# Another written-out order for the attention steps, with two more tiles of exponentials and the splitting of the maxima moved to GpSimd

## Chip, core and metric

The kernel runs on one core of a Trainium2 chip. The metric is the device time of one execution in microseconds (us). Engines are called as the profile calls them: PE (matmuls), DVE (VectorE), ACT (ScalarE), POOL (GpSimd), SP (the queue that issues most DMAs). Engines run side by side, each one its own instructions in order, and they wait for each other by semaphores.

## What is computed

From one input x of 2048 tokens by 512 features the kernel computes a gate, a sliding-window attention and an MLP, and mixes them:

```python
def _A_ref(x, wqkv, wo):        # 32 heads of 16, window of 256
    qkv = (lambda x, *d: x.transpose(*d))((x @ wqkv).reshape(B, S, 3, H, Dh), 2, 0, 3, 1, 4)
    scores = jnp.einsum("bhqd,bhkd->bhqk", q, k) * (Dh ** -0.5)
    mask = (idx[:, None] - idx[None, :] >= 0) & (idx[:, None] - idx[None, :] < W)
    scores = jnp.where(mask[None, None], scores, -1e9)
    p = _softmax(scores, axis=-1)
    o = jnp.einsum("bhqk,bhkd->bhqd", p, v)
    return (lambda x, *d: x.transpose(*d))(o, 0, 2, 1, 3).reshape(B, S, D) @ wo

def _B_ref(x, w1, b1, w2, b2):  # layer norm, 512 -> 1792, gelu, -> 512
    h = _gelu(jnp.einsum("bsd,df->bsf", _layernorm(x), w1) + b1)
    return jnp.einsum("bsf,fd->bsd", h, w2) + b2

g = _sigmoid((x * gate_w).sum(-1, keepdims=True))
return g * a + (1 - g) * b
```

All products are made with numbers split into a high and a low part, so that one product is three matmuls (or, in the scores, one matmul over stacked rows of high and low parts).

## The kernel before, in words

There are three stages, and PE has matmuls in all of them.

**Projections (to about 158 us).** q, k and v are made from x; q and k go through DRAM into "stacks", the tiles `q` and `k` of two heads per half, whose rows hold high and low parts. Here too the first maxima of the attention are made, while DVE and POOL prepare the normalised input `y` of the MLP.

**Attention mixed with the first MLP layer (about 158 to 520 us).** The 32 heads are done in eight passes of four heads (two tiles `q`, `k` with two heads each). PE's order in this stage is a string written out by hand, `ORDER`, with a letter for each step; `run` takes the letters one after the other:

- **S** (`s_pair`, L311): the scores of 128 queries with up to 384 keys, for two heads (two matmuls that run side by side, L322). DVE then masks two edges into one (`copy_predicated`, L331) and takes the row maxima (`tensor_reduce`, L332). For the first two blocks of a pass another DVE operation does it (L328).
- After the second S of every fourth block `put_max` (L336) splits four blocks' negated maxima into a high and a low part (L340, L341), transposes them on DVE (L342), writes them to DRAM (`md`, L352, one tick later) and reads them back as two more rows of `q` (L350, three ticks later). A tick is one step of a clock of the program, which `block` moves on at each T with `pr` 0. The rows of `k` that meet these rows of `q` hold 1.0 (L181), so that the matmul itself subtracts the maximum.
- **T** (`st_pair`, L357): the same scores transposed, keys by queries, with the maximum subtracted (L366). ACT takes the exponential into a tile `p` (L368), and POOL zeroes the corners outside the window (`affine_select`, L370, two for a full T). One tile `p` serves the two T of a block of keys; five are there.
- **P** (`pv`, L377): probabilities times v for 256 queries (32 matmuls of 32 columns in the trace, 16 for the first P of a pass, L385). ACT copies the result out (L121, in the last ones DVE, L392). A P reads the tiles `p` of its own two blocks of keys and of the two blocks before.
- **f** (`fill`, L655): one step, two matmuls side by side, of the first MLP layer (`mlp1_unit`, L561, matmul L575). 24 such steps make a unit of 128 hidden features by 1024 tokens; ACT copies its two halves out, and it goes to DRAM as `hp`.

PSUM, where matmuls write, has four places in this stage, the tiles `b0` to `b3` (two banks each). `ring` hands them out: the unit of the MLP holds one through its 24 steps, and S, T and P take the other three in turn. So the place that an S has written is free for the third S, T or P behind it, and that one's matmul waits until DVE (or ACT) has emptied it.

**Second MLP layer and output (from about 520 us).** The rest of the f, the second layer (L783), the output projection (L762) and the mix.

SP issues the loads and stores in the order of the program: weights of the MLP at each unit's end, stacks of the next pass (L309) and the transfers of `put_max` by ticks.

Of the kernel before, what the change touches and what calls it, by code (L numbers as in the profile page):

```python
# [17 lines left out]
ALU = mybir.AluOpType  # L18
# [11 lines left out]
NB = S // 128  # L30
# [4 lines left out]
EPS = 1e-5  # L35
NEG = -3.0e38
U8 = mybir.dt.uint8
ORDER = ("fSfTffSPffTfSffTfSffTfTfffSfTffSffSfffSPSffTfSffTfSffTfffTSPSfSfTfffTfffTSfTfffSfSPSTfTSfTffffSTPSTf"
         "TffSffTfSffTPSfTfTfffSfTffSffSPSfTfffTfSfTfffSfTPTfSfTfffTfSfTffSffTSfffSPTSfTffSffTPTSffTfSfTfSffSP"
         "SfTfSffTfTfSTfffTfSfSfPTSffTfSfTfSffTPTSfTffSfTfSffTPTSfTffTffSfTffSffSPSfTSfffTfSffTfSffTfffSTPTSff"  # L40
         "TfSffTfSffffSfSPTffTfSffTfffSfTPSfTfSfffTfSffTfSffTffSffSPSTffSffTfTffSfTfffTffSPTfSfTffSfffTfSfffSP"
         "TfSfTffSfTffTfSPTfSfTffSffTfSffTfSffTffSffSPTSfTfffTfSPSffTfSffTfSffTffSffTfSffTffSffSPTSTfffSffTPTf"
         "SfTffSffTSffTfSffSPTfSfTffTfffSfSPSffTfSffTfSffTfSfffTSffTfffSTPSfTfSffTfSffSPTSfTffSffTfSffTfffTTPT"
         "fTfSffTfffTfSPTSfTffSffSPSfTSfffTfSffTffTfSfTfffTfSPSfTffSffTffSffSPTSfTfffTfSfTfffSfTPTSfTffSffTfSf"
         "fTfSffTfSffSPTSfTfffSfTfffTfSPTfSfTfffSffTfffSTPTSfTfffSfSPSffTffTfSffTffSffTfSffTfSffffSfTffSffSPSf"
         "TfffTfSfTffSffTPTfSfTffSfffTfSffTfSfffSPTfSffTfffTfSPTfSfTfffSfTffSffTfSffTffSffSPTSfTfffSfTPTfSfTff"
         "SffTfffSTPTfSffTfSffTfSfffSPTSffTfSfTfSffTfSffTSffSPTSffTfSffTffTfSfTffSfSPTfSfTffSffTTfffSPTfSffTfS"
         "ffTffTfSfffSfffSPTfSfTffSffTfSffTfSfffSPTfSfTffTffSfTfffSfSPTSTffffTSPTSfTfffTfSfTffTffSPTSfTffSffTS"
         "ffTfSffSPTSTfffSffTPTSfTffSffTSffTfSffSPSTfSTSTfTffTPTTffffTfPTfffTffTfffTffTPTffTffffTfTPTTfffffTTP"
         "TfT")  # L50
LAG = 6


# [1 line left out]
def gated_mix_kernel(ctx, tc: tile.TileContext, xt, x2, wqk, wv, wo, xa, gw, w1, w2, b1, b2, out):  # L55
    nc = tc.nc
    dve, act, pool, pe, sp = nc.vector, nc.scalar, nc.gpsimd, nc.tensor, nc.sync
# [5 lines left out]
    def nm(s):  # L63
        uid[0] += 1
        return f"{s}_{uid[0]}"
# [10 lines left out]
    def get(key, tag, bufs, shape, dt=F32):  # L76
        return left[key].tile(list(shape), dt, name=nm(tag), tag=tag, bufs=bufs)
# [48 lines left out]
    def after(k, fn):  # L126
        todo.setdefault(step[0] + k, []).append(fn)
# [49 lines left out]
    def masks():  # L177
        for t in qs + ks:
            pool.memset(f32(t[:32]), 0.0)
        for k in ks:  # L180
            pool.memset(f32(k[96:128]), 1.0)  # L181
        one = small("scr", 2, (128, 256), BF16)
        pool.memset(one, 1.0)
        pool.affine_select(out=one[:, :128], in_=one[:, :128], pattern=[[-1, 128]], base=0, channel_multiplier=1,
                           compare_op=ALU.is_ge, fill=0.0)
        for e in range(2):
            pool.tensor_copy(tri[:, e], one[:, :128])
        pool.memset(wide, 0.0)
        pool.affine_select(out=wide[:, 128:], in_=wide[:, 128:], pattern=[[-1, 128]], base=0, channel_multiplier=1,
                           compare_op=ALU.is_ge, fill=NEG)  # L190
# [145 lines left out]
    def put_max(p, a):  # L336
        mx = mxs[p][:, :, :, a:a + 4]
        m = small("nm", 2, (128, 2, 2, 2, 4), F32R)
        ms = small("ms", 2, (128, 32))
        dve.tensor_scalar(m[:, 0], mx, -1.0, None, op0=ALU.mult)  # L340
        dve.scalar_tensor_tensor(out=m[:, 1], in0=mx, scalar=-1.0, in1=f32(m[:, 0]), op0=ALU.mult, op1=ALU.subtract)  # L341
        dve.transpose(ms, f32(m).rearrange("p a b c d -> p (a b c d)"))  # L342
        md = dram.tile([2, 2, 2, 4, 128], F32R, name=nm("md"))

        def rest():
            done.add(("m", p, a // 4))
            for pr in range(2):
                for e in range(2):
                    src = view(md, [2048, 2], [1, 512], off=(2 * pr + e) * 512)
                    sp.dma_start(f32(qs[pr][62 + 50 * e:64 + 50 * e, a * 128:a * 128 + 512]), f32(src))  # L350

        after(1, lambda: sp.dma_start(f32(view(md, [32, 4], [128, 32], [1, 32])), ms))  # L352
        after(2 if (p, a) == (7, 12) else 3, rest)

    pts, acc = {}, {}

    def st_pair(p, kb, pr):  # L357
        w = min(NB - kb, 3) * 128
        assert ("m", p, (kb * 128 + w - 1) // 512) in done
        if pr == 0:  # L360
            pts[p, kb] = get("work", "p", 5, (128, 4, 384))
        pt = pts[p, kb][:, 2 * pr:2 * pr + 2]
        o = two()
        for e in range(2):
            r, k = ((0, 64), (64, 114))[e]
            pe.matmul(o[:, e, :w], ks[pr][r:k, kb * 128:kb * 128 + 128], qs[pr][r:k, kb * 128:kb * 128 + w],  # L366
                      start=True, stop=True)
        act.activation(pt[:, :, :w], o[:, :, :w], AF.Exp, scale=0.25)  # L368
        for a, sgn, b in ((0, 1, 0), (256, -1, -1))[:1 + (w == 384)]:
            pool.affine_select(out=pt[:, :, a:a + 128], in_=pt[:, :, a:a + 128], pattern=[[0, 2], [sgn, 128]],  # L370
                               base=b, channel_multiplier=-sgn, compare_op=ALU.is_ge, fill=0.0)
# [5 lines left out]
    def pv(p, j, last):  # L377
        flush()
        a = two()[:, 0]
        parts = ((-1, 0, 128, 256), (-2, 0, 256, 128), (0, 0, 0, 256), (1, 128, 0, 128))[0 if j else 2:]  # L380
        for n, (d, at, fr, w) in enumerate(parts):
            kb = 2 * j + d
            for h in range(4):
                v = (4 * p + h) * VW
                pe.matmul(a[32 * h:32 * h + 32, at:at + w], vs[:, kb, v:v + 32], pts[p, kb][:, h, fr:fr + w],  # L385
                          start=n == 0, stop=n == len(parts) - 1, skip_group_check=True, tile_position=(0, 32 * h))
        if j % 2 == 0:
            acc[p] = t2()
        s = acc[p]
        o = j % 2 * 256  # L390
        if last:
            dve.tensor_copy(s[:, o:o + 256], a[:, :256])  # L392
        else:
            copy(s[:, o:o + 256], a[:, :256])
        if j % 2:
            to = osc[p, :, (j - 1) * 256:(j + 1) * 256]
            if lt:
                after(1, lambda: sp.dma_start(to, s))
            else:
                act.dma_start(to, s)  # L400
# [263 lines left out]
    early = []  # L664
    lt = [(p, kb, pr) for p in range(8) for kb in range(NB) for pr in range(2)]
    ls = [(p, qb, pr) for p in range(8) for qb in range(NB) for pr in range(2)][2 * (NB - LAG):]
    lp = [None] + [(p, j) for p in range(8) for j in range(NB // 2)]

    def run(order):
        for a in order:  # L670
            flush()
            if a == "T":
                p, kb, pr = lt.pop(0)
                if not pr:
                    block(p, kb)
                st_pair(p, kb, pr)
            elif a == "S":
                s_pair(*ls.pop(0))
            elif a == "P":
                a = lp.pop(0)  # L680
                if a:
                    pv(*a, not ls)
            else:
                fill()

    run(ORDER)
    flush()
# [108 lines left out]
    for n in range(len(seq)):  # L796
        tick()
        for k in (n + 6,):
            c, f = item(k)
# [4 lines left out]
        c, f = item(n + 1)  # L804
# [6 lines left out]
        c, f = seq[n]  # L811
# [5 lines left out]


def build():
    nc = bacc.Bacc("TRN2", target_bir_lowering=False, num_devices=1)  # L820

    def inp(name, shape):
        return nc.dram_tensor(name, list(shape), F32, kind="ExternalInput").ap()

    args = [inp("in_xt", (NCH, 128, DT * C)), inp("in_x2", (2, 128, KT * C)), inp("in_wqk", (NG, 2, 128, DT * 128)), inp("in_wv", (DT, 128, D)),
            inp("in_wo", (DT, 128, D)), inp("in_xa", (NB, 128, D)), inp("in_gw", (D,)),
            inp("in_w1", (FT, 128, D)), inp("in_w2", (FT, 128, D)), inp("in_b1", (128, FT)), inp("in_b2", (D,))]
    out = nc.dram_tensor("out", [NB, 128, D], F32, kind="ExternalOutput").ap()
    with tile.TileContext(nc) as tc:
        gated_mix_kernel(tc, *args, out)  # L830
    if not nc.is_finalized():
        nc.finalize()
    return nc
# [28 lines left out]
```

## Time and profile before

| what | us |
|---|---|
| median of the runs | 731.01 (730.85 to 731.36, three runs) |
| the profiled execution | 736.04 |
| its span, first to last instruction | 734.3 |
| PE busy in the span | 710.0 |
| DVE, ACT, POOL busy | 491.6, 370.7, 269.2 |
| first step of ORDER to the last P (about 158 to 520) | 362.2 |

The granted clock of PE was 0.993 over the span. The profile counts a matmul as busy from its start to an end that it models, so that two matmuls that overlap in the pipeline hide short waits between them; the start times of the matmuls show such waits, the busy share doesn't.

### The profile page before, as it was taken

To read this page: it belongs to the slowest core of one execution; us is meant where nothing else is said; L and a number is where in the kernel's file an instruction comes from. 1 tells how busy PE (TensorE), PEld (TensorE's weight loads), DVE (VectorE), ACT (ScalarE), POOL (GpSimd) and SP (SyncE) were. 2 spreads that over 40 slices of the span, in tenths; PEclk is the share of its full clock that TensorE was granted. 3 is DMA by queue.
4 is the path that set the end of the run, shared out by engine and by line. 5 is a ranking of instruction groups with operands and counts; after the bars stand their busy time and mean duration, and the time that the engine had idled before them with its cause. 6 is when DMAs were issued, how large, how long until landed. Compare 5 with 4: busy or idle time off the path is not lost.

```text
span 734.3 us, 16117 instructions
## 1 busy us (share of the span) xinstructions
PE 710.0 (97%) x5728; PEld 541.6 (74%) x5728; DVE 491.6 (67%) x1045; ACT 370.7 (50%) x584; POOL 269.2 (37%) x548
## 2 busy tenths in 40 slices
PE   6899999999999999999999999999999999999997
PEld 5577777777766767777777777766777788888886
DVE  4427885878877867886778788785374745735554
ACT  4432122357658657666776767667653413224121
POOL 9040005768747446455663556456300000000000
PEclk9999999999999999999999999999999999999999
DMA  8999857786666775647765644634585544442531
GB/s 290 285 303 285 253 157 234 228 239 208 202 186 183 237 221 172 189 129 237 232 178 171 198 144 140 193 105 148 179 280 155 172 134 143 146 137 97 185 110 57
DMA packets 104675, 138.46 MB, mean 189 GB/s; under 512 B 15668, under 2 KB 55540, under 8 KB 104468
## 3 DMA queue, kind: packets, MB, share of 16 engines
q1 hardware_dynamic: 97540, 125.11, 55.1%
q10 hardware_dynamic: 7056, 12.32, 5.2%
q8 instruction: 46, 0.75, 0.4%
q14 instruction: 33, 0.27, 0.1%
HBM read 82.06 MB, written 54.28 MB: 186 GB/s over the span
## 4 chain that ended last, share of the span: by engine, by line
PE 80%; DMA 8%; DVE 5%; SPq 2%; ACT 2%; issue 2%; ACTq 1%; POOL 0%; DVEq 0%
PE ps_b L575 18%; PE ps_a L783 16%; PE ps_b L385 11%; PE ps_d L272 10%; PE ps_b L366 8%; PE ps_b L322 6%; PE ps_o L762 6%; PE ps_d L297 5%; DVE mx L332 2%; DMA t<-in_w 2%; DVE ps_b L331 1%; DMA t<-in_wv 1%; DMA t<-in_wqk 1%; DMA osc<-t 1%; DMA qk<-t 1%
## 5 line engine op out<-in xcount | busy, mean ns | idle before, releaser
L370 POOL TENSOR_SCALAR_AFFINE_SELECT p<-p 128x256 f32<-128x256 f32 x480 | 184.1, 413 | 147.5 <-ACT p L368 143.8
L575 PE MATMUL ps_b<-x,w 64*128 64x512 f32 x1344 | 223.8, 396 | 0.1
L368 ACT ACTIVATE p<-ps_b 128x768 f32<-128x768 f32 (+2 forms) x256 | 191.8, 772 | 60.5 <-PE ps_b L366 53.5
L783 PE MATMUL ps_a<-x,t 128*128 128x512 f32 x648 | 154.4, 395 | 0.1
L332 DVE TENSOR_REDUCE mx<-ps_b 128x2 f32<-128x512 f32 x208 | 144.0, 693 | 7.2
L783 PEld LDWEIGHTS ps_a<-x,t 128*128 128x128 f32 x648 | 121.5, 188 | 30.0 <-DVE t L118 0.8
L575 PEld LDWEIGHTS ps_b<-x,w 64*128 64x128 f32 x1344 | 132.6, 187 | 8.8 <-DVE t L392 0.4
L331 DVE COPY_PREDICATED ps_b<-tri,ps_b 128x256 f32<-128x256 uint8 x208 | 88.2, 424 | 48.6 <-PE ps_b L322 45.2
L366 PE MATMUL ps_b<-q,k 64*128 64x384 f32 (+5 forms) x512 | 97.6, 366 | 6.6 <-DVE mx L332 1.8
L272 PE MATMUL ps_d<-x,w 128*128 128x512 f32 x360 | 92.0, 404 | 4.7 <-ACT x L121 3.5
L385 PE MATMUL ps_b<-p,v 128*32 128x128 f32 (+1 forms) x1920 | 92.6, 332 | 0.3 <-DVE mx L328 0.2
L322 PE MATMUL ps_b<-k,q 62*128 62x384 f32 (+2 forms) x472 | 88.4, 352 | 1.6 <-DVE mx L332 1.2
L272 PEld LDWEIGHTS ps_d<-x,w 128*128 128x128 f32 x360 | 67.9, 191 | 24.4 <-ACT x L121 5.3
L385 PEld LDWEIGHTS ps_b<-p,v 128*32 128x32 f32 x1920 | 54.2, 110 | 36.2 <-ACT p L368 7.4
L366 PEld LDWEIGHTS ps_b<-q,k 64*128 64x128 f32 (+1 forms) x512 | 52.5, 185 | 38.5 <-PE ps_b L322 16.2
L121 ACT ACTIVATE t<-ps_b 128x256 f32<-128x256 f32 (+1 forms) x114 | 52.9, 489 | 51.7 <-PE ps_b L385 42.4
L322 PEld LDWEIGHTS ps_b<-k,q 62*128 62x128 f32 (+1 forms) x472 | 48.7, 185 | 19.7 <-PE ps_b L366 5.1
L118 DVE TENSOR_TENSOR t<-t,t 128x512 fp32r<-128x512 f32 x70 | 48.5, 692 | 14.6 <-ACT t L121 11.6
L463 POOL TENSOR_TENSOR t<-t,t 128x512 f32<-128x512 f32 x16 | 22.9, 1432 | 76.4 <-DVE ps_x L331 73.1
L631 ACT ACTIVATE t<-t,b1s 128x512 f32<-128x512 f32 x56 | 37.9, 715 | 25.5 <-DMA t<-hp 25.0
L121 ACT ACTIVATE t<-t 128x512 fp32r<-128x512 f32 x16 | 10.1, 632 | 78.3 <-DVE t L750 49.8
L762 PE MATMUL ps_o<-w,t 128*128 128x512 f32 x192 | 46.6, 391 | 0.8 <-ACT t L121 0.8
(71 smaller groups left out, 541.4 us busy)
## 6 DMA issues: line engine op xcount, KB each, us to landing
t<-hp SPq DMA_DIRECT2D x56, 256.0 KB
hp<-t SPq DMA_DIRECT2D x52, 256.0 KB
k<-qk SPq DMA_DIRECT2D x112, 98.0 KB
q<-qk SPq DMA_DIRECT2D x112, 98.0 KB
qk<-t ACTq DMA_DIRECT2D x40, 256.0 KB
qk<-t SPq DMA_DIRECT2D x32, 256.0 KB
osc<-t SPq DMA_DIRECT2D x31, 256.0 KB
t<-in_w SPq DMA_DIRECT2D x28, 256.0 KB
```

Of the source, the lines that this page charges most:

```text
L121: act.activation(dst, src, AF.Copy)
L272: pe.matmul(o, a[:, dt * 128:(dt + 1) * 128], b[:, dt * C:(dt + 1) * C], start=n == 0, stop=n == 11)
L322: pe.matmul(o[:, e, :n], qs[pr][r:k, qb * 128:qb * 128 + 128], ks[pr][r:k, t0:t0 + n], start=True, stop=True)
L331: dve.copy_predicated(o[:, :, :128], tri, o[:, :, 256:384])
L332: dve.tensor_reduce(m, o[:, :, :256], mybir.AxisListType.X, ALU.max)
L366: pe.matmul(o[:, e, :w], ks[pr][r:k, kb * 128:kb * 128 + 128], qs[pr][r:k, kb * 128:kb * 128 + w], start=True, stop=True)
L368: act.activation(pt[:, :, :w], o[:, :, :w], AF.Exp, scale=0.25)
L370: pool.affine_select(out=pt[:, :, a:a + 128], in_=pt[:, :, a:a + 128], pattern=[[0, 2], [sgn, 128]], base=b, channel_multiplier=-sgn, comp ...
L385: pe.matmul(a[32 * h:32 * h + 32, at:at + w], vs[:, kb, v:v + 32], pts[p, kb][:, h, fr:fr + w], start=n == 0, stop=n == len(parts) - 1, sk ...
L575: pe.matmul(o[:, e], w[kt // 4][r:r + 64, k, m:m + 128], y[r:r + 64, a:a + C], start=n == 0, stop=n == 23)
L762: pe.matmul(a, x[:, g], wos[g][:, k], start=n == 0, stop=n == 11)
L783: pe.matmul(accs[c][b], x[:, b * 128:(b + 1) * 128], w, start=f == 0 and n == 0, stop=f == FT - 1 and n == 2)
```

## The change

```diff
-ORDER = ("fSfTffSPffTfSffTfSffTfTfffSfTffSffSfffSPSffTfSffTfSffTfffTSPSfSfTfffTfffTSfTfffSfSPSTfTSfTffffSTPSTf"
...
+ORDER = ("fSfTfffffTfTSfffSffTfSfffTTfffTfSfffSPSTSfffTTfffSfffTSfffTffSfTPTSffTffSffTSffSfSPTSTfffSffTfSffSPT"
...
         for k in ks:
-            pool.memset(f32(k[96:128]), 1.0)
+            pool.memset(f32(k[96:128]), -1.0)
...
-        dve.tensor_scalar(m[:, 0], mx, -1.0, None, op0=ALU.mult)
-        dve.scalar_tensor_tensor(out=m[:, 1], in0=mx, scalar=-1.0, in1=f32(m[:, 0]), op0=ALU.mult, op1=ALU.subtract)
-        dve.transpose(ms, f32(m).rearrange("p a b c d -> p (a b c d)"))
+        pool.tensor_copy(m[:, 0], mx)
+        lo_part(m[:, 1], mx, m[:, 0], pool)
         md = dram.tile([2, 2, 2, 4, 128], F32R, name=nm("md"))
+
+        def turn():
+            dve.transpose(ms, f32(m).rearrange("p a b c d -> p (a b c d)"))
+            sp.dma_start(f32(view(md, [32, 4], [128, 32], [1, 32])), ms)
...
-        after(1, lambda: sp.dma_start(f32(view(md, [32, 4], [128, 32], [1, 32])), ms))
+        after(1, turn)
         after(2 if (p, a) == (7, 12) else 3, rest)
...
-            pts[p, kb] = get("work", "p", 5, (128, 4, 384))
+            pts[p, kb] = get("work", "p", 7, (128, 4, 384))
...
-    lp = [None] + [(p, j) for p in range(8) for j in range(NB // 2)]
+    lp = [(p, j) for p in range(8) for j in range(NB // 2)]
...
-                a = lp.pop(0)
-                if a:
-                    pv(*a, not ls)
+                pv(*lp.pop(0), not ls)
...
-    nc = bacc.Bacc("TRN2", target_bir_lowering=False, num_devices=1)
+    nc = bacc.Bacc("TRN2", target_bir_lowering=False, num_devices=1, dynamic_dma_scratch_size=1024)
```

- The order string is another one. Both hold 647 f, 256 T and 236 S, and 63 P that do something (the first P of the old string was an empty one); the last P and 25 f stand behind the string in both.
- Seven tiles `p` instead of five; the room (two tiles of 6,144 bytes in each partition) comes from the scratch of the DMA, cut to 1024. All DMAs of this program are issued from SP and ACT.
- The maximum is no longer negated: the rows of `k` hold -1.0. So the high part is a plain copy and the low part a difference, and POOL makes both. DVE keeps the transpose, which moves one tick on, to the place where SP gets the write to `md`.

On PE the change shows in the seventh pass (p = 6), around the last S of its third group of four blocks; k_6 and q_4 are the stacks of the second pair of heads, p_... the tiles of exponentials. Before:

```order
L322 MATMUL ps_b_1052_6415<-k_6_82,q_4_80 128x384 x2
L575 MATMUL ps_b_1035_6291<-x_273_1549,w_5157 128x512 x2
L575 MATMUL ps_b_1035_6291<-x_232_1312,w_5156 128x512 x2
L366 MATMUL ps_b_1056_6430<-q_4_80,k_6_82 128x384 x2
L575 MATMUL ps_b_1035_6291<-x_232_1312,w_5156 128x512 x4
L366 MATMUL ps_b_1058_6446<-q_3_79,k_5_81 128x384 x2
L575 MATMUL ps_b_1035_6291<-x_232_1312,w_5156 128x512 x2
L322 MATMUL ps_b_1059_6454<-k_5_81,q_3_79 128x384 x2
L575 MATMUL ps_b_1035_6291<-x_274_1550,w_5157 128x512 x2
L366 MATMUL ps_b_1060_6461<-q_4_80,k_6_82 128x384 x2
```

and of the change:

```order
L369 MATMUL ps_b_1051_6402<-q_4_80,k_6_82 128x384 x2
L322 MATMUL ps_b_1052_6408<-k_6_82,q_4_80 128x384 x2
L578 MATMUL ps_b_1033_6271<-x_232_1312,w_5131 128x512 x4
L578 MATMUL ps_b_1033_6271<-x_272_1538,w_5132 128x512 x2
L369 MATMUL ps_b_1057_6431<-q_3_79,k_5_81 128x384 x2
L578 MATMUL ps_b_1033_6271<-x_272_1538,w_5132 128x512 x4
L322 MATMUL ps_b_1058_6441<-k_5_81,q_3_79 128x384 x2
L578 MATMUL ps_b_1033_6271<-x_272_1538,w_5132 128x512 x2
L322 MATMUL ps_b_1064_6456<-k_6_82,q_4_80 128x384 x2
L388 MATMUL ps_b_1065_6461<-p_6230,v_83 32x256 x4
```

Before, T and S alternate with one or two f (a row x4 is two f) between. In the change a T and an S stand directly behind each other more often (87 T with an S right behind them, 35 before) with two or three f behind the pair, and the P of the pass before (L388) comes here, two blocks of keys later than before.

On DVE, at the same place, `put_max` stood as three operations between the reduce of the last S and the work of the next S:

```order
L331 COPY_PREDICATED ps_b_1052_6415<-tri,ps_b_1052_6415 128x2x128
L332 TENSOR_REDUCE mx_5858<-ps_b_1052_6415 128x2
L340 TENSOR_SCALAR nm_6420<-mx_5858 128x16
L341 SCALAR_TENSOR_TENSOR nm_6420<-mx_5858,nm_6420 128x16
L342 STREAM_TRANSPOSE ms_6421<-nm_6420 128x32
L331 COPY_PREDICATED ps_b_1059_6454<-tri,ps_b_1059_6454 128x2x128
```

and stands as one:

```order
L331 COPY_PREDICATED ps_b_1052_6408<-tri,ps_b_1052_6408 128x2x128
L332 TENSOR_REDUCE mx_5858<-ps_b_1052_6408 128x2
L345 STREAM_TRANSPOSE ms_6414<-nm_6413 128x32
L331 COPY_PREDICATED ps_b_1058_6441<-tri,ps_b_1058_6441 128x2x128
L332 TENSOR_REDUCE mx_5858<-ps_b_1058_6441 128x2
```

No S stands between the last S of the group and the transpose here, nor in 22 others of the stage's 30 groups; in seven one to three do. What it reads, `nm`, now comes from POOL, where the two operations stand between the corners of the T before the S and of the T behind it:

```order
L373 AFFINE_SELECT p_6393<-p_6393 128x2x128 x4
L340 CAST nm_6413<-mx_5858 128x16
L118 TENSOR_TENSOR nm_6413<-mx_5858,nm_6413 128x16
L373 AFFINE_SELECT p_6430<-p_6430 128x2x128 x4
```

So two of DVE's three operations became two of POOL's, and between reduce and transpose there are now two hand-overs, from DVE to POOL and back.

More of the change, by code (lines that the diff above doesn't have):

```diff
@@ L37 @@
 U8 = mybir.dt.uint8
-ORDER = ("fSfTffSPffTfSffTfSffTfTfffSfTffSffSfffSPSffTfSffTfSffTfffTSPSfSfTfffTfffTSfTfffSfSPSTfTSfTffffSTPSTf"
[L39 to L50, printed above, removed]
@@ new lines @@
+ORDER = ("fSfTfffffTfTSfffSffTfSfffTTfffTfSfffSPSTSfffTTfffSfffTSfffTffSfTPTSffTffSffTSffSfSPTSTfffSffTfSffSPT"
+         "fTSfffTffTfSfTffSfffTSfffSPSTSPTffTSffTffTffTfTfSfSPSffTSfffTfSffTfSffTSffSPTSTPSTSffffTSfffTfSffTfS"
+         "fffTSffffTSffTfffSfSPTSTPTSffTfffTSffTffTffTSffTffSfSPTffTfSfTffSffSPSTSPSffTfSffTfSfffTfSffTfSffffT"
+         "SfffTfSfffSPSTSPTffTSffTffSffTfSfffTSfffTfSffTPTSffTffSffSPffTTSffffTffSTffTffSfTffSffTSfffTfSfffSPS"
+         "TTPTSTPSffTfSfffTSfffTfSffTfSfffTSfffTfTfffSfSPffTfTSffffTSffTfSfffSPfTSfffTfSffTfSfffSPTSfTffSffTSf"
+         "ffTfSffTfSfffTSffTfSffTfSfffSPPSSTPTSffTffSffTfSfffTSfffTfSfffTfSffTfSfffSPSTSPfTffTSffTffffSTPfTSfT"
+         "fffTffTSffTffTffTSffSPSTSPTSffTffSffTSffffTSfffTfSfffTSfffTfSffTPfSTPSffTfSfffTSfffTfSffTfSffTfSffTf"
+         "SffTfSffSPSTTPfTSfTfffTffTSffTfffTfSPfTSffTffSffTSffffSPSTSPfTffTSffTfSffffTSfffTfSffTfSfffTSfffSfPf"
+         "SfTfPfSTfffSfffTfSffTfSfffTSfffTfSfffSPfTSfTfffTffSTfffSffTSfffTfSffTfSffTfSffSPTSffTffSffSPSfTfSfff"
+         "TSfffTfSffTfSfffTSfffSPTTSPTSffTffTffTfTfSffTfSfffTSfffSPTfTSfffTffSfSPSTfTfffTSfffTfSffTfSfffTSfffT"
+         "fSfffTSfffSPSTSPTTSPTSTPTSfffTfSfffTfSffTfSfffTSfffTfSffTfSfffSPSTSPfSffTSffffTSfffTffTffTSffTffSffT"
+         "SffffSPTTSPSfTSffffTSfffTffTfSfTfffTffTSfffTffSfTPfSTPTSTPfTffTffTffTfTfPfTTPTfTfffTffTTfffTfPffTTPf"
+         "TT")
```

## The prediction

> **What bounds the kernel now.** I read the busy line first, then the stretch of the attention, then the chain of waits through it. The busy line, and the attention from 158 to 520 us (length, then busy time by engine):
>
> ```profile
> PE 710.0 (97%) x5728; PEld 541.6 (74%) x5728; DVE 491.6 (67%) x1045; ACT 370.7 (50%) x584; POOL 269.2 (37%) x548
> sum 362.20, PE 353.65 PEld 261.27 DVE 278.04 ACT 250.37 POOL 208.98; mean PE 44.21 PEld 32.66 DVE 34.76 ACT 31.30 POOL 26.12
> ```
>
> PE seems to leave 8.6 us of the attention idle. But overlapping matmuls hide waits, so I count by starts. What one step takes with nothing in its way stands in the chain of waits (start, length, what):
>
> ```profile
> 308.99 0.03 PE ps_b L366
> 309.02 0.79 PE ps_b L385 x16
> 449.55 0.18 PE ps_b L322 x2
> 450.63 0.70 PE ps_b L575 x6
> 451.54 1.44 PE ps_b L385 x32
> ```
>
> Three f take 0.70, so one is 0.233 us; an S or T of full width 0.18; a P 1.44, the first of a pass 0.79. The old order has 647 f (150.8), 55 long and 8 short P (85.5), 432 full S and T (77.8) and 60 narrow ones, at half a full one by estimate (5.4): 319.5 us of 362.2. The other 43 us are waits and edges. Some stay: switching to P's weights and back costs about a quarter of a us by the starts around P, and there are 63 P in either order, 16 us. So some 27 us are to be had at most. Where does the chain go when it leaves PE? Its shares in the attention, and one place:
>
> ```profile
> by line: PE ps_b L575 36.6%; PE ps_b L385 22.6%; PE ps_b L366 15.5%; PE ps_b L322 11.9%; DVE mx L332 3.7%; DVE ps_b L331 2.4%; issue 2.2%; DMA osc<-t 1.6%; DMA q<-md 1.1%; ACT p L368 0.8%; DVE nm L340 0.5%; SPq L288 0.3%; ACT t L121 0.2%; D
> 443.49 0.70 DVE mx L332
> ...
> 444.22 0.19 DVE nm L340
> ...
> 444.43 0.19 DVE nm L341
> ...
> 444.64 0.21 DVE ms L342
> 444.85 0.35 DVE ps_b L331
> ...
> 447.40 0.70 DVE mx L332
> 448.10 0.14 issue
> 448.24 0.44 PE ps_b L322 x2
> ```
>
> From 443.49 to 448.24 DVE works without a pause: four reduces, and the three operations of the maxima between the first and the second. The S at 448.24 needs the PSUM place that the last reduce frees. The row of that S in the timeline, and two rows of the waits of PE (total, times, longest):
>
> ```profile
> 448.24 0.44 PE L322 MATMUL ps_b<-k,q 62*128 62x384 f32 x2 [0.33 <-DVE mx L332]
> PE ps_b L366 <- DVE mx L332: 1.8, 5, 0.5
> PE ps_b L366 <- DMA q<-md: 1.6, 1, 1.6
> ```
>
> By its start this S is 0.50 us late, not 0.33. Setting every late S, T or P against the end of the DVE work on its place, in the timeline, I find **14.2 us of lateness in 59 places, all behind an S's place**. 4.2 us of it falls within 4.2 us behind the last reduce of a `put_max` group; 9.9 us has other causes, S too close together. These two and the 1.6 us for rows of `q` are what the change can touch. No P is late by the exponentials or corners: a long P lasts 1.44 almost everywhere. So the two more tiles `p` give nothing alone; they let the order move P.
>
> **The change, part by part.** *The order.* An S holds its place for what DVE does:
>
> ```profile
> L332 DVE TENSOR_REDUCE mx<-ps_b 128x2 f32<-128x512 f32 x208 | 144.0, 693 | 7.2
> L331 DVE COPY_PREDICATED ps_b<-tri,ps_b 128x256 f32<-128x256 uint8 x208 | 88.2, 424 | 48.6 <-PE ps_b L322 45.2
> ```
>
> 0.42 + 0.69 = 1.11 us, with the hand-overs some 1.4 to 1.6 from the S's last column to the next writer's start. The order alone tells what time PE has to fill before it comes to that writer. With the step times above, from the end of an S to the next writer of its place: before, a median of 1.51 us where a T writes and 1.64 where an S does, and 52 of 236 under 1.5; in the change 1.74 and 1.80, and 17 of 236 under 1.5. What is missing sums, against 1.5 us, to 11.8 before and 3.3 after, against 1.6 to 23.5 and 6.7: 28% of before in both. So of the 9.9 us I keep 2.8: **-7.1 us**. Bounds: -9.9 if all have room, 0 if S that follow each other closely (68 runs of six S in under 5.8 us of PE work, 56 before) let DVE fall behind instead.
>
> *The maxima.* Their rows by tile (shortest, median, longest ns), a place where one is long, and what bounds the same on POOL:
>
> ```profile
> L340 DVE TENSOR_SCALAR nm<-mx x32: 174/175/1268, 85.3 to 500.3; 128x16 fp32r<-128x16 f32 x32
> L341 DVE SCALAR_TENSOR_TENSOR nm<-mx,nm x32: 174/286/1216, 85.5 to 500.5; 128x16 fp32r<-128x16 f32 x32
> L342 DVE STREAM_TRANSPOSE ms<-nm x32: 211/211/214, 85.8 to 500.8; 128x32 f32<-128x32 f32 x32
> 456.06 1.29 POOL L118 TENSOR_TENSOR w<-t,w 128x512 fp32r<-128x512 f32 x1
> 456.11 1.27 DVE L340 TENSOR_SCALAR nm<-mx 128x16 fp32r<-128x16 f32 x1
> L820 POOL MEMSET const-float32-1.0<- 128x1 f32 x1 | 0.1, 99 | 0.0
> L118 DVE TENSOR_TENSOR t<-t,t 128x512 fp32r<-128x512 f32 x70 | 48.5, 692 | 14.6 <-ACT t L121 11.6
> L370 POOL TENSOR_SCALAR_AFFINE_SELECT p<-p 128x256 f32<-128x256 f32 x480 | 184.1, 413 | 147.5 <-ACT p L368 143.8
> L368 ACT ACTIVATE p<-ps_b 128x768 f32<-128x768 f32 (+2 forms) x256 | 191.8, 772 | 60.5 <-PE ps_b L366 53.5
> ```
>
> Today the group holds DVE for 0.56 us at least, 0.8 to 0.9 typically. In the change DVE does 0.21, but waits first, and the next S's work is queued behind the waiting transpose. POOL's two operations of 16 columns are not in the trace; they lie between the memset (0.10 us) and a select (0.41) each; I take 0.15, nearest to the small one, 0.3 for both. With 0.2 for the hand-overs the hold is 0.7 if POOL is free. In 15 of the 30 groups a T stands directly before the S, and its exponential (0.81) and two selects (0.82) end some 0.4 us after the reduce: 1.1 there, so **0.9 on the mean, as today**. But nine groups have the next S within 1.33 us, six before. I scale 4.2 by 1.3 to 5.4: **+1.2 us**. Bounds: -4.2, and +14 if POOL answers late (a rival).
>
> The Trainium skill speaks against this move: GPSIMD Engine Reference, section 4.1 Engine selection, sends elementwise work to VectorE and has GPSIMD about twice as slow on two inputs; 1.29 against the 0.69 of DVE's same form agrees. Section 3.1 has 2.6 cycles per element beside a dispatch; by it the pair would take some 0.4 us (an estimate), the hold 1.0 and the sum 0.5 more.
>
> *Rows of `q`.* The one wait of 1.6 us comes from transfers that SP issued late:
>
> ```profile
> 248.72 5.74 DMA osc<-t
> 254.47 0.55 SPq L288
> 255.06 0.60 SPq L288
> 255.76 4.11 DMA q<-md
> ```
>
> Nothing in the change keeps SP clear there, but the coincidence need not recur; I take half, **-0.8 us** (-1.6 to +1.6). The transfers themselves come later now, by POOL and the tick. Write and read-back of the maxima on SP, where the second waits for the first:
>
> ```profile
> 490.99 0.53 SPq L352 DMA_DIRECT2D md<-ms  x1
> 492.93 1.14 SPq L350 DMA_DIRECT2D q<-md  x4
> ```
>
> From an S's end to rows in place: 1.4 (DVE), 0.7, 1.9, 1.1, and 1.9 for the landing, taken like the first: 7.0. The orders leave 8.4 us or more of PE work before, and in the change 6.5 at the last group of the last pass, 9.0 or more elsewhere. **+0.7 us** there (0 to 2).
>
> *At nothing:* the -1.0 in `k` and the smaller scratch change no instruction that takes time; POOL's wait for the reduce delays selects, which P, a median 5.3 us behind its last T (2.0 before), covers; without that cover it is 0.4 a group.
>
> The sum: -7.1 + 1.2 - 0.8 + 0.7 = **-6.0 us**, all in the attention; what follows starts from its last P and moves along. The profiled execution took 736.04 us, 5.0 above the median of the runs; the sum makes it 730.0, and on the median of 731.0 it makes **725.0 us**.
>
> **Rivals.** *More than that.* If the new order was spaced for DVE's whole queue, and POOL answers while DVE still waits for an S, all 14.2 us shrink to the 3.3 of the count: -10.9, and -1.6 for the rows of `q`: 718.5. For it: DVE waits for S often now (45.2 us in its row above), and L340 beside POOL's work took 1.27 instead of 0.17, which DVE no longer suffers. The Trainium skill (SBUF — State Buffer, Who interferes with whom) calls this an exclusive lock between the two engines; by it the hold today is 0.2 longer than DVE's own work, which the move ends. Against it: the nine close S.
>
> *Slower: POOL answers late.* The place is the transpose, with no S between it and the reduce in 23 groups. If a hold is b instead of 0.9, and it reaches PE where the next S is close (nine of 23, 0.4), the cost is 23 x 0.4 x (b - 0.9). It eats the 6.0 from b = 1.55. That takes an ACT that is behind by one exponential, or the 1.29 us of a weight's low part ahead on POOL (12 in the kernel). At b = 2.0 it is +10.1, or 735.1.
>
> *Nothing.* S come in tighter runs, DVE (77% busy here) falls behind, and the 7.1 us come back as waits a few steps later; with the small terms +1.1: 732, or about 731 if half the gain for `q` is whole.
>
> **How the numbers follow.** Forecast (722 to 728) 0.45; more 0.28; nothing 0.13; slower 0.14. A measurement of this kernel tells 0.2% (1.5 us) from no change. Faster: 0.45 + 0.28 and a little of the third, 0.77; same 0.10; slower 0.13. The range leaves a tenth on each side: from 716.5, below the second case, to 732.0, the third.
>
> **What would show it.** In the changed profile the chain should spend under 4% of the attention on DVE lines (6.6% now), the attention should be 356 us long, DVE's busy sum there lower by some 15, and late S and T behind an S's place should sum to about 8 us. A wait of the transpose for POOL of over 1 us in most groups, with S late behind it, shows the slower rival; lateness moved to ACT's places or to rows of `q` shows that the count by places was too narrow.

## The result and the profile after

The changed kernel takes **728.02 us** (median of 22 runs, 725.85 to 734.51); the old one, run beside it, 731.84 (22 runs, 729.22 to 737.82). The ratio is 0.9954 with an interval of 0.9941 to 0.9968, so by the ratio 3.4 us or 0.46% faster (the medians differ by 3.8). A second measurement gave 0.995 (0.9934 to 0.9967). The direction was forecast and the time lies in the range, but the gain is little more than half of the 6.0 us that the sum gave.

The profiled execution took 728.15 us, close to its median. Its span and busy line, then the attention from 156.2 to 512.2 us in the same columns as before (sum of the stretch, busy time of each engine, and means; PEld are PE's loads of weights):

```profile
span 726.4 us, 16108 instructions
PE 699.0 (96%) x5728; PEld 542.1 (75%) x5728; DVE 472.7 (65%) x981; ACT 370.3 (51%) x584; POOL 281.1 (39%) x612
sum 356.00, PE 344.30 PEld 262.79 DVE 259.09 ACT 250.53 POOL 220.02; mean PE 344.30 PEld 262.79 DVE 259.09 ACT 250.53 POOL 220.02
```

DVE's sum in the attention fell by 19 us (15 forecast), POOL's rose by 11; that is the split of the maxima on its new engine. The stretch is 356.0 long, the very figure forecast. But the execution of before that I started from was itself some 5 us above the median of its runs, and this one is at its median: the pair flatters the change. Where the chain of waits goes in that stretch ("issue" is time in which an engine waited for nothing that the profile shows):

```profile
by line: PE ps_b L578 32.4%; PE ps_b L388 21.6%; PE ps_b L369 11.4%; PE ps_b L322 10.2%; DVE mx L332 3.6%; POOL p L373 3.2%; DVE ps_b L331 2.5%; issue 2.3%; DMA q<-md 1.7%; ACT p L371 1.7%; DMA t<-in_w 1.1%; DMA q<-qk 1.0%; DMA k<-qk 1.0%; 
```

DVE's two lines on S (L332, L331) have 6.1%, just what they had before (the 6.6% of the prediction holds L340's 0.5% too); under 4% was forecast for DVE's lines. S still wait for their place. The share is a rough sign, though: in the profile of the order alone, below, the two lines have 2.8%, with as much lateness. New on the chain are POOL's corners (L373, 3.2%) and more transfers, and ACT's exponentials have twice their share (0.8% before, 1.7% now). The rows of the waits of PE there:

```profile
PE ps_b L369 <- DVE mx L332: 3.3, 7, 1.1
PE ps_b L369 <- DMA q<-md: 2.9, 1, 2.9
PE ps_b L322 <- DVE mx L328: 1.5, 2, 1.3
...
PE ps_b L322 <- DMA q<-qk: 0.5, 1, 0.5
```

**The maxima.** The operations on `nm` (shortest, median, longest ns), and who waited for them:

```profile
L340 POOL CAST nm<-mx x32: 191/196/201, 83.4 to 495.8; 128x16 fp32r<-128x16 f32 x32
L118 POOL TENSOR_TENSOR nm<-mx,nm x32: 220/221/223, 83.7 to 496.1; 128x16 fp32r<-128x16 f32 x32
  POOL nm L118: 17.1, 22
```

The two take 0.196 and 0.221 us where I had estimated 0.15 each. DVE waits for them in 22 of the stage's 30 groups, 17.1 us in all, 0.78 each; with the transpose's own 0.21 the hold of DVE in these 22 is 1.0 on the mean, against 0.9 forecast. One of the long ones, in the timeline of all engines:

```profile
270.30 0.69 DVE L332 TENSOR_REDUCE mx<-ps_b 128x2 f32<-128x512 f32 x1
270.36 1.48 POOL L373 TENSOR_SCALAR_AFFINE_SELECT p<-p 128x256 f32<-128x256 f32 x4 [2.86 <-ACT p L371]
271.79 0.20 POOL L340 CAST nm<-mx 128x16 fp32r<-128x16 f32 x1
272.07 0.22 POOL L118 TENSOR_TENSOR nm<-mx,nm 128x16 fp32r<-128x16 f32 x1
272.33 0.21 DVE L345 STREAM_TRANSPOSE ms<-nm 128x32 f32<-128x32 f32 x1 [1.33 <-POOL nm L118]
272.46 0.25 DVE L328 CUSTOM_DVE_ANT_0 scr<-ps_b,wide 128x128 bf16<-128x128 f32 x1
272.99 0.33 PE L322 MATMUL ps_b<-k,q 62*128 62x128 f32 x2 [0.26 <-DVE mx L328]
```

The reduce ends at 270.99. POOL is in its selects until 271.79, since they waited 2.86 us for an exponential; so the transpose starts 1.33 us late, and the next S's work (L328), ready all the while, stands queued behind it. The S at 272.99 needed the place that L328 frees. This is the rival "POOL answers late" at one group: it is real, but of the 22 waits four are over 1 us and thirteen the least that is seen, 0.60.

### The profile page after: what moved, and what is told of

Its sections match the earlier page's. It is cut to its first block, busy times and chain, and to the rows that moved or that the text cites. A ratio compares the mean times of both kernels' runs of the same rounds, so it can differ in the third digit from the quotient of the medians.

```text
span 726.4 us, 16108 instructions
## 1 busy us (share of the span) xinstructions
PE 699.0 (96%) x5728; PEld 542.1 (75%) x5728; DVE 472.7 (65%) x981; ACT 370.3 (51%) x584; POOL 281.1 (39%) x612
## 4 chain that ended last, share of the span: by engine, by line
PE 78%; DMA 7%; DVE 5%; POOL 3%; SPq 2%; ACT 2%; issue 2%; ACTq 1%; DVEq 0%; POOLq 0%
PE ps_b L578 17%; PE ps_a L784 16%; PE ps_d L272 11%; PE ps_b L388 11%; PE ps_o L763 6%; PE ps_b L369 6%; PE ps_d L297 5%; PE ps_b L322 5%; DVE mx L332 2%; DMA qk<-t 2%; POOL p L373 2%; DVE ps_b L331 1%; DMA t<-in_w 1%; PE ps_d L260 1%; DMA hp<-t 1%
## 5 line engine op out<-in xcount | busy, mean ns | idle before, releaser
L373 POOL TENSOR_SCALAR_AFFINE_SELECT p<-p 128x256 f32<-128x256 f32 x480 | 184.2, 413 | 116.7 <-ACT p L371 115.0
L578 PE MATMUL ps_b<-x,w 64*128 64x512 f32 x1344 | 216.8, 398 | 0.5 <-DVE mx L332 0.4
L332 DVE TENSOR_REDUCE mx<-ps_b 128x2 f32<-128x512 f32 x208 | 144.1, 693 | 7.2
L331 DVE COPY_PREDICATED ps_b<-tri,ps_b 128x256 f32<-128x256 uint8 x208 | 88.1, 424 | 54.9 <-PE ps_b L322 46.4
L369 PE MATMUL ps_b<-q,k 50*128 50x384 f32 (+5 forms) x512 | 91.8, 346 | 7.1 <-DVE mx L332 3.3
L388 PE MATMUL ps_b<-p,v 128*32 128x128 f32 (+1 forms) x1920 | 91.3, 329 | 0.7 <-ACT p L371 0.5
L322 PE MATMUL ps_b<-k,q 62*128 62x384 f32 (+2 forms) x472 | 86.9, 346 | 3.5 <-DVE mx L328 1.5
L388 PEld LDWEIGHTS ps_b<-p,v 128*32 128x32 f32 x1920 | 54.1, 109 | 36.8 <-ACT p L371 4.8
L322 PEld LDWEIGHTS ps_b<-k,q 62*128 62x128 f32 x472 | 48.2, 186 | 17.5 <-ACT p L371 4.0
L297 PE MATMUL ps_d<-wv,x 128*128 128x512 f32 x192 | 46.9, 394 | 0.0
```

Of the source, the lines that this page charges most:

```text
L297: pe.matmul(o, x[:, a:a + 128], wvs[dt][:, k], start=n == 0, stop=n == 11)
L322: pe.matmul(o[:, e, :n], qs[pr][r:k, qb * 128:qb * 128 + 128], ks[pr][r:k, t0:t0 + n], start=True, stop=True)
L331: dve.copy_predicated(o[:, :, :128], tri, o[:, :, 256:384])
L332: dve.tensor_reduce(m, o[:, :, :256], mybir.AxisListType.X, ALU.max)
L578: pe.matmul(o[:, e], w[kt // 4][r:r + 64, k, m:m + 128], y[r:r + 64, a:a + C], start=n == 0, stop=n == 23)
```

## Experiments

All ratios are to the old kernel, with 95% intervals. "Lateness" is counted as in the prediction: by how much an S, T or P starts later than the steps before it would let it, where it starts right behind the end of the work on its PSUM place (counted the same way for every trace, the old kernel has 14.8 us behind S's places, 4.9 of it behind `put_max`; the prediction's own count had 14.2 and 4.2). "Attention" is from the start of the first f to the start of the last P: 362.1 us in the profiled execution of before, 354.6 in that of after.

### Taking the change apart

**Order alone.** The new order and seven tiles, but the maxima split on DVE and `k` with +1.0 as in the old kernel:

```diff
-        pool.tensor_copy(m[:, 0], mx)
-        lo_part(m[:, 1], mx, m[:, 0], pool)
+        dve.tensor_scalar(m[:, 0], mx, -1.0, None, op0=ALU.mult)
+        dve.scalar_tensor_tensor(out=m[:, 1], in0=mx, scalar=-1.0, in1=f32(m[:, 0]), op0=ALU.mult, op1=ALU.subtract)
+        dve.transpose(ms, f32(m).rearrange("p a b c d -> p (a b c d)"))
```

> The new order and the seven tiles, with the split of the maxima on DVE as before (negated, ones in k). My theory: the order is what gains, and POOL's answer (the transpose waited 17.1 us for it in 22 groups) gives DVE no time back. Then this is as fast as the whole change or up to 1 us faster: ratio to before 0.994 to 0.996, and S, T or P late behind an S's place sums to 9 to 11 us. Rival, the move to POOL carries the gain because DVE is the bound: 0.998 to 1.001.

Measured: 727.77 us, ratio 0.9962 (0.9942 to 0.9982). That is the whole gain of the change, within the interval: the order makes it. Lateness behind S's places is 10.8 us (7.6 behind `put_max`, 3.2 elsewhere), against 14.8 in the old kernel and 10.4 in the changed one. This profile has a late T too, 2.6 us behind its rows of `q`, and half clock after it, at the same step as the changed kernel: that wait comes with the order, not with POOL's split or the later transpose.

**The split alone.** The old order and five tiles, with POOL's split, the later transpose and -1.0:

```diff
-        after(1, lambda: sp.dma_start(f32(view(md, [32, 4], [128, 32], [1, 32])), ms))
+        after(1, turn)
```

> The old order and five tiles, with the split of the maxima on POOL, minus ones in k and the transpose a tick later. My theory: a hold of DVE of about 1.0 us stands in place of one of 0.9, so nothing or a small loss: 1.000 to 1.002. Rival, the move to POOL carries the gain: 0.996 to 0.998.

Measured: 735.12 us, ratio 1.004 (1.0018 to 1.0062): **slower**. Not for DVE's hold, since lateness behind S's places is as before (14.7; 4.8 of it behind `put_max`). Its waits of PE name the cause, and the stretch around it (start and end, length, then busy us and instructions of PE, PEld, DVE, ACT, POOL; then the granted clock, the DMA share and GB/s) shows a sequel:

```profile
PE ps_b L369 <- DMA q<-md: 3.0, 1, 3.0
349.30:352.80 3.50, 0.51 (x5) 0.15 (x2) 1.33 (x3) 0.65 (x1) 1.86 (x6) 1.00 0.87 296
352.80:356.30 3.50, 3.50 (x22) 2.72 (x26) 0.49 (x2) 1.62 (x2) 1.16 (x4) 0.52 0.67 218
```

A T stands 3 us for its rows of `q`. Their write to `md` goes out at 343.9, 4.7 us behind the group's last reduce; in tiles alone, which has the same order and the split on DVE, that is 3.2 us and the T stands 1.5. And then the clock is at half for 3.4 us: PE issues 22 matmuls in 3.5 us, some 50 are usual.

**Tiles alone.** The old kernel with seven tiles and the small scratch:

```diff
-            pts[p, kb] = get("work", "p", 5, (128, 4, 384))
+            pts[p, kb] = get("work", "p", 7, (128, 4, 384))
```

> The old order and the old split, with seven tiles of exponentials and the small DMA scratch. My theory: no P waits for a tile and no T for room that matters (3.1 us of waits of ACT for POOL's tiles in all), so 0.9995 to 1.0005. Rival, the tiles or the scratch matter: a ratio off 1 by over 0.002.

Measured: 732.96 us, ratio 1.0013 (0.9999 to 1.0027): nothing that is clear of the noise. Its attention of 360.0 us is the better one to compare with, for its mean granted clock (0.997) is that of the execution below (0.996).

**The changed kernel again**, to tell what recurs from what is chance:

> The changed kernel itself, for a second profile and its ratio on this chip. Expected: 0.9941 to 0.9968, the attention 354 to 356 us long by starts, and, if the two longer waits in the second MLP layer (1.4 and 0.7 us) belong to the change and not to one execution, the same two waits again; if they are chance, none.

Measured: 728.64 us, ratio 0.995 (0.9934 to 0.9967); attention 354.1. The wait for rows of `q` came again at the same step, 2.46 us (3.05 in the first profile). A wait of 1.2 us in the second layer did not, so that one is chance.

### The rows of `q`

**Read back a tick earlier** in the changed kernel:

```diff
-        after(2 if (p, a) == (7, 12) else 3, rest)
+        after(2, rest)
```

> The changed kernel with the read-back of the maxima into the rows of q issued two ticks behind their group instead of three. My theory: the T of pass 1 at 232 us waits 2.5 to 3.0 us for these rows in all three profiles of the new order because SP issues them late (6.4 us behind the reduce); a tick earlier this wait goes: 2 to 3 us less than the changed kernel, ratio to the old one 0.991 to 0.993. Rival: SP blocks on the landing of the write instead and holds the loads behind it, no gain: 0.994 to 0.997.

Measured: 727.09 us, ratio 0.9922 (0.9893 to 0.995). The wait of that T is gone, but others came: three S are late for their stacks, the longest 1.34 us. So the lateness moved in part. The profiled execution, 729.45 us, is the slowest of the six, and its attention of 354.4 is no shorter than that of the changed kernel.

**The same edit with the old order and the split on POOL:**

```diff
+        after(1, turn)
-        after(2 if (p, a) == (7, 12) else 3, rest)
+        after(2, rest)
```

> The old order with the split on POOL (1.004 in the run before) and the read-back a tick earlier. My theory: that kernel lost its 2.9 us by rows of q that come late (a T waited 3.2 us for them), not by DVE; with the earlier read-back it is level with the old kernel: 0.999 to 1.001. Rival, DVE's wait for POOL costs it: 1.003 to 1.005 again.

Measured: 733.71 us, ratio 1.0014 (0.9994 to 1.0034) where the split alone had 1.004, and no T waits for rows in its profile. So most of what the split alone loses is the late rows, though the two intervals overlap a little.

**Stores out of the way.** Why are the rows late in the changed kernel? SP's timeline ahead of them, and the chain of waits up to the T:

```profile
222.75 0.60 SPq L346 DMA_DIRECT2D md<-ms  x1
...
226.18 0.37 SPq L485 DMA_DIRECT2D t<-in_w  x1
226.65 0.85 SPq L591 DMA_DIRECT2D hp<-t  x2
227.59 0.45 SPq L401 DMA_DIRECT2D osc<-t  x1
228.09 1.51 SPq L353 DMA_DIRECT2D q<-md  x4
```
```profile
225.76 0.39 ACT t L121
226.15 1.56 ACT p L371 x2
227.70 0.34 SPq L401
228.04 0.05 issue
228.09 4.28 DMA q<-md
232.37 0.14 issue
232.50 0.68 PE ps_b L369 x2
```

The write to `md` went out at 222.75, but the read-back is issued only at 228.09: ahead of it in SP's queue stand four copies for the stacks, a load and three stores, and the chain has the last store wait for ACT until 227.70. The rows land at 232.37, and T starts at 232.50. But the queue was no emptier in the old kernel. SP's timeline of before, at the same group:

```profile
225.39 0.59 SPq L352 DMA_DIRECT2D md<-ms  x1
...
230.47 1.33 SPq L350 DMA_DIRECT2D q<-md  x4
```

That is 5.1 us between write and read-back, and no wait, since the T came 11.4 us after the group's last S. In the new order 9.1 us of work lie between the two (late stores, below, where this T is on time). I moved the stores one tick back:

```diff
-                after(1, lambda: sp.dma_start(to, s))
+                after(2, lambda: sp.dma_start(to, s))
...
-                after(1, lambda: sp.dma_start(hp[2 * cp + e, f], s))
+                after(2, lambda: sp.dma_start(hp[2 * cp + e, f], s))
```

> The changed kernel with SP's stores of attention and MLP results (osc, hp) one tick later, so that SP doesn't stand waiting for ACT's copies with the read-back of the maxima behind it. My theory: the new order lost some 2 to 4 us by the T at 230 us that waits 2.5 to 3.3 us for rows of q, and by the 3.4 us of half clock that follow such a wait in most executions; here the wait falls under 1 us, no window of half clock stands in the attention, and the ratio to the old kernel is 0.990 to 0.993 (changed kernel 0.995). Rival: another transfer makes PE wait instead, 0.994 to 0.997.

Measured: 727.2 us, ratio 0.9925 (0.9897 to 0.9952); attention 352.1, 2.0 to 2.5 less than in the two profiles of the changed kernel. The read-back goes out 4.2 us behind its write instead of 5.3, and the T starts on time 2.5 us behind that issue, so the rows for it land faster too (4.28 above). In time the two kernels' intervals overlap. The two stretches around the place, after and then late stores:

```profile
229.30:232.60 3.30, 0.43 (x6) 0.13 (x2) 0.00 (x0) 1.38 (x3) 2.81 (x6) 1.00 0.70 232
232.60:236.10 3.50, 3.50 (x20) 3.38 (x20) 1.27 (x3) 1.62 (x2) 1.27 (x4) 0.52 0.67 209
```
```profile
229.30:232.60 3.30, 3.00 (x28) 2.06 (x24) 1.57 (x4) 3.22 (x5) 3.17 (x7) 1.00 0.84 289
232.60:236.10 3.50, 3.50 (x52) 2.68 (x52) 2.53 (x6) 1.83 (x3) 2.51 (x9) 1.00 0.83 250
```

The pause is gone, and the half clock behind it with it. Now two short waits are left: an S for its stack (0.38), and a T for rows (0.79) at the last group of pass 7, which the prediction named.

### The place of the transpose

**Late turn.** The changed kernel, but the transpose and its write stand behind DVE's work on the next S, if one comes within two ticks:

```diff
+        last_turns()
...
+    turns = []
+
+    def last_turns():
+        while turns:
+            turns.pop(0)()
...
-        after(1, turn)
+        if (p, a) == (7, 12):
+            after(1, turn)
+        else:
+            turns.append(turn)
+            after(2, last_turns)
```

> The changed kernel with the transpose (and the write to md) behind DVE's work on the next S, so that POOL's answer is there when DVE comes to it. My theory: DVE's 17.1 us of waiting for POOL goes to under 2, and of the 6.2 to 6.5 us of lateness behind these groups half goes: 2 to 3 us less than the changed kernel, 0.991 to 0.993. Rival: DVE's hold is not what makes those S late, or the later write makes rows of q late instead: 0.994 to 0.998.

Measured: **721.89 us**, ratio 0.9857 (0.9824 to 0.9889): a gain of 10.5 us by the ratio, three times that of the change and twice and more what I expected, and the lowest median of the study. What waits for `nm`, the chain through the attention, and the same group as above:

```profile
  POOL nm L118: 6.0, 11
```
```profile
by line: PE ps_b L589 36.2%; PE ps_b L399 22.3%; PE ps_b L380 12.1%; PE ps_b L322 11.1%; POOL p L384 3.1%; ACT p L382 1.8%; issue 1.5%; DMA t<-in_w 1.3%; DMA md<-ms 1.2%; DVE mx L332 1.2%; DMA k<-qk 1.2%; DMA q<-md 1.1%; DVE ps_b L331 0.8%;
```
```profile
267.68 0.29 DVE L328 CUSTOM_DVE_ANT_0 scr<-ps_b,wide 128x128 bf16<-128x128 f32 x1 [0.42 <-PE ps_b L322]
...
268.59 0.21 DVE L352 STREAM_TRANSPOSE ms<-nm 128x32 f32<-128x32 f32 x1 [0.41 <-POOL nm L118]
...
268.83 0.23 PE L322 MATMUL ps_b<-k,q 62*128 62x128 f32 x2
```

DVE does L328 at once, then turns, and the S at 268.83 carries no wait. Lateness behind S's places falls from 10.4 to 5.8 us, that behind `put_max` from 6.2 to 2.2; DVE's two lines are 2.0% of the chain, not 6.1%. Attention: 349.4, which is 5.2 less than in the first profile of the changed kernel. Late rows and stacks shrink with it, from 3.8 us to 1.7, and lateness behind ACT's places grows, from 2.7 to 5.1; so the gain is not the maxima's alone.

**Late turn with the early read-back** (both edits):

```diff
+            after(2, last_turns)
-        after(2 if (p, a) == (7, 12) else 3, rest)
+        after(2, rest)
```

> Both edits of the changed kernel, the transpose behind the next S and the read-back a tick earlier. If both theories hold and add up: 0.987 to 0.990. If one undoes the other (SP waits for the later write): no better than the better of the two.

Measured: 734.35 us, ratio 1.0025 (1.0007 to 1.0044), **12 us worse** than the late turn alone. S are as little late as there (5.6), but rows and stacks are late again, and its clock is 0.99:

```profile
PE ps_b L380 <- DMA q<-md: 3.9, 4, 2.6
PE ps_b L322 <- DMA q<-qk: 2.4, 2, 1.6
```

The write leaves a tick later and the read is queued a tick earlier, so SP waits for the write's landing with everything behind it in its queue. SP's own waits show it (total, times, longest), first here, then in the late turn alone:

```profile
SPq L360 <- DMA md<-ms: 52.4, 29, 3.9
SPq L360 <- DMA md<-ms: 26.3, 21, 2.2
```

In the changed kernel this wait is 3.1 us in all. How much of the 12 us it makes, no run separates.

**Late turn with late stores** (both edits as above):

```diff
+            after(2, last_turns)
...
+                after(2, lambda: sp.dma_start(to, s))
```

> The same later stores on top of the transpose behind the next S (which alone had 0.986). If the two causes are separate: 0.981 to 0.984. If what the later transpose gained was this same wait for rows of q: 0.985 to 0.988.

Measured: 722.69 us, ratio 0.9881 (0.985 to 0.9912); attention 348.5. No better than the late turn alone: that kernel has only 1.71 us of late rows left to remove. By the expectation this is the second case: part of what the late turn gains is the same wait for rows of `q`.

**Late split on DVE.** Is it the engine or the place in the queue? The new order, all three operations on DVE, but behind the next S's work:

```diff
+        def turn():
+            dve.tensor_scalar(m[:, 0], mx, -1.0, None, op0=ALU.mult)
+            dve.scalar_tensor_tensor(out=m[:, 1], in0=mx, scalar=-1.0, in1=f32(m[:, 0]), op0=ALU.mult, op1=ALU.subtract)
             dve.transpose(ms, f32(m).rearrange("p a b c d -> p (a b c d)"))
```

> The new order with the whole split on DVE, as in the old kernel, but behind the next S's work. No POOL, no wait on it; DVE works some 0.6 us a group more than with POOL's help. My theory, that the place of the hold counts and not the engine: near the kernel with the later transpose, 0.986 to 0.990. Rival, that taking the two operations off DVE is what gained there: 0.993 to 0.997, near the order alone (0.996).

Measured: 727.43 us, ratio 0.994 (0.9919 to 0.9961), no better than the change: my theory failed, and the rival's forecast holds. Behind the next S the three are in the way of the one after:

```profile
270.46 0.42 DVE L350 TENSOR_SCALAR nm<-mx 128x16 fp32r<-128x16 f32 x1
270.92 0.32 DVE L351 SCALAR_TENSOR_TENSOR nm<-mx,nm 128x16 fp32r<-128x16 f32 x1
271.27 0.21 DVE L352 STREAM_TRANSPOSE ms<-nm 128x32 f32<-128x32 f32 x1
```

They hold DVE for 1.0 us here, from 270.46 to 271.48 (0.65 by the medians of the three). Lateness behind `put_max` is 8.6, the highest of all. So both are needed: POOL to take the work off, and the place in DVE's queue to hide POOL's answer.

**Late turn in the old order** (split on POOL as above):

```diff
+            turns.append(turn)
+            after(2, last_turns)
```

> The old order with the split on POOL and the transpose behind the next S. In the old order 4.9 us of lateness lie behind these groups. If the hold of DVE is a cause of its own: 2 to 4 us less than POOL's split alone (1.004), so 0.998 to 1.001. If the later write to md makes rows of q late in this order, as they were with POOL alone: 1.003 to 1.006.

Measured: 733.81 us, ratio 1.0035 (1.0011 to 1.0059). Lateness behind `put_max` falls only from 4.8 to 3.5, for less was there; a T waits 3.1 us for rows of `q` at 351.3, as in the split alone. As built, the late turn pays in the new order only; the old order with its rows in time was not tried with it.

## Why the prediction came out half right

Held against the two profiles with like clocks, tiles alone (360.0) and the changed kernel again (354.1), the attention is 5.9 us shorter, almost the forecast 6.0. But that is luck: what the prediction gave terms for (order, maxima, rows of `q`) comes to some -2.3 there, and edges that it put at nothing bring most of the rest. The sizes found below add up to about -4.8 for this pair; 1.1 us is not placed. And 5.9 is not the gain of the timed runs.

- **The order, far from `put_max`: forecast -7.1, found -5.4 to -5.7.** 9.9 us went to 4.3 (in the second pair of profiles 9.7 to 4.3), so 43% stayed where the count by the order had 28%. The mechanism holds.
- **The maxima: forecast +1.2, found +1.1 to +1.3.** 4.9 went to 6.2 (5.4 to 6.5). The hold of 0.9 measured 1.0. That the sizes agree is in part chance. In the order alone, with the split left on DVE, 4.9 went to 7.6 behind `put_max` and 9.9 to 3.2 elsewhere; the move to POOL then took 1.4 off the one and added 1.0 to the other (one profile each). So the order makes this term, and POOL's part is a gain that the 1.3 of the prediction did not hold. What I missed most is that the term need not be there: the transpose can stand behind the next S's work, and then 4.0 us go. The rival "more than that" had the gain in sight (S late by 3.3 us in all, 718.5) but not what it took.
- **Rows of `q`: forecast -0.8 and +0.7, found +2.0 (with the stacks, 1.73 in tiles alone, 3.69 in the changed kernel again).** This is the step that failed. I set 7.0 us from an S's end to its rows in place, and so found too little PE work at the last group of pass 7 only, and the 9.0 elsewhere enough. At the group of pass 1 the way took 12.0: 1.3 to the end of the reduce, 1.1 to the write, 5.3 to the read-back, 4.3 to the landing. With 9.1 us of work to cover it, that leaves the 3.0 that the T waits. Two parts of my sum were wrong, and the old profile had both: the 1.9 from write to read-back is the shortest of its 32 (the median is 3.5, and this group had 5.1), and 1.1 and 1.9 for issue and landing make 3.0 where the row of `q<-md` that I showed says 4.11. POOL and the tick, which I blamed for later transfers, are not the cause: the order alone has the same late T (2.6 us). The two kernels without this wait, late stores and the read-back a tick earlier, have ratios of 0.9925 and 0.9922, some 2 us below the change; each interval overlaps the change's, so the size in the timed runs is not sharp. In late stores the attention is 2.0 to 2.5 us shorter.
- **The clock: forecast nothing.** The first profile pays for the pause with 3.4 us at half clock. By the step times against the second profile this is about 1.3 us (the steps f and their edges take so much longer). The timed runs bear on it, if not from one series: of the old kernel's 23 runs beside the order alone, 19 were granted 0.997 or more, of the changed kernel's first 22 only 11. These 11 have a mean of 727.4, the 19 of the old kernel 732.0, which is -4.6, some 1 us more than the medians show.
- **Edges: forecast nothing, found -4.5 and +0.9.** The steps around S and T that wait for nothing (place, rows, P) held 9.8 us more than their natural time, now 5.3; S and T directly next to each other now cost 0.9 more. In the old timeline, from an S to the f behind it:

```profile
448.49 0.42 PE L575 MATMUL ps_b<-x,w 64*128 64x512 f32 x2
...
449.36 0.37 PE L322 MATMUL ps_b<-k,q 62*128 62x384 f32 x2
449.54 0.66 PE L575 MATMUL ps_b<-x,w 64*128 64x512 f32 x4
```

  The S at 448.24, which the prediction shows as late, is followed by its f after 0.25 us; the S on time at 449.36 after 0.18. So a late S costs its lateness and some 0.07 on the f (the six S of before that are over 0.15 us late and have an f behind them have a median of 0.25, the others 0.18). The new order has fewer late steps, and fewer such switches at all (578 steps in this class, 674 before). That these two make up the whole 4.5 is not shown. I had counted what steps take on time only. P's own edges, 16 us by estimate, hardly moved, as forecast: with P's waits for its place 9.7 before and 9.5 after above its natural time.
- **ACT's places: forecast nothing, found +1.3 to +2.0** (1.7 to 3.0 in the second pair, 0.7 to 2.7 in the first). T and P now come close behind the exponentials, 5.1 us with the late turn. "Lateness moved to ACT's places or to rows of `q`" was named as the sign that the count by places was too narrow, and both are seen.
- **At nothing**: seven tiles and scratch, nothing (1.0013, its interval includes 1).
- **Slower rival.** At single groups it is there (1.33 us above), but the hold is 1.0 on the mean; its break-even of 1.55 was far.

What stays open: the timed gain (-3.4 and -3.7 by the two ratios) is smaller than the -5.9 of the pair of profiles; the one was 1.6 us above its own median, the other 2.2 below, and why single runs differ in that way was not settled. Nor was why late stores, without the pause, still had runs at 0.992 to 0.994 of the clock. ACT's places were not tried by themselves, nor SP's DMAs of L288 beside the late rows.

## What to carry to other kernels

An operation that waits for another engine is to be put behind the next independent work of its own queue: as the change had it, the split on POOL brought nothing measurable beside the order alone; with the transpose put there, 6 to 7 us more, some of which is rows of `q` that came in time. When a transfer starts later, look at what stands ahead of its issue in the DMA queue's engine and waits there for data, not only at how much work lies between issue and use; and take the time of a transfer from the place in question, or the median, not from the shortest in the trace. A count of free room by order alone gave the main term to within a quarter; the errors lay in the resources that the count did not hold.

## What the runs showed of the hardware

**A pause of PE for some 3 us is followed by half clock.** Count a pause from one matmul's start to the next, in the attention of all profiles. Five of five pauses of 2.8 us or more (2.80 to 3.39, all for rows of `q`) are followed by a stretch of 3.4 us with a granted clock of 0.5, once of 6.8 us (the late turn with the early read-back): as above at 349.3 us of the split alone and at 229.3 of after. Of eleven pauses of 1.9 to 2.7 us, two are. The changed kernel again, where PE stood 2.67 us at the same step, kept its clock:

```profile
232.60:236.10 3.50, 3.50 (x48) 2.69 (x51) 2.62 (x6) 1.63 (x2) 1.70 (x5) 1.00 0.67 228
```

48 matmuls here, 20 in the same stretch of after. One window of before (at 499.6 us) has no such pause ahead of it. The Trainium skill (TensorE: Matmul & The Clock Gate, What's actually happening) has the clock fall to half after at least one idle window of about 3.4 us, with free-running windows; the length of the stretches agrees (3.41 us each, or twice that). Windows that run freely would let pauses of one length come out either way, as they do here. But pauses shorter than a window, two of them of only about 2.0 us, were enough.

**A small operation on POOL is not much longer than on DVE:** 0.196 and 0.221 us for 128x16 on POOL against 0.174 and 0.174 at the shortest on DVE. What the move costs is the way there and back: 0.60 us from the reduce's end to the transpose's start at the least.
